# Sketched attention and a tanh-shrink FFN: weight loads cast by GpSimd's DMAs, fillers planned at the cold clock, more loads in flight

## The chip, the cores and the metric

The kernel runs on one core of a Trainium2 chip. The metric is device time in microseconds (us) of one execution, as the median of several. Shorter is better. The engines are TensorE (PE in the profile; PEld is its weight load), VectorE (DVE), ScalarE (ACT), GpSimd (POOL) and SyncE (SP). They run side by side, each through its own list of instructions in order, and wait for one another by semaphores. DMAs are issued by SP, ACT or POOL and carried out by 16 DMA engines that all of them share.

## The reference, cut to what matters

There are 4 batches of 4 heads, 1088 tokens each, 32 values per head. Queries and keys are sketched by two 8x32 matrices; the feature map is the outer product of the two sketches (64 features). Attention is linear: one 64x32 matrix per head is made from all keys and values, and each query is multiplied by it and divided by a denominator. The result, 4352 tokens x 128 values, goes through an FFN of width 2048.

```python
def phi(x):
    a = np.einsum('rd,bhsd->bhsr', S1, x)
    b = np.einsum('rd,bhsd->bhsr', S2, x)
    return np.einsum('bhsi,bhsj->bhsij', a, b).reshape(*x.shape[:-1], r * r)
q_p, k_p = (phi(q), phi(k))
kv = np.einsum('bhsf,bhsd->bhfd', k_p, v)
z = np.sum(k_p, axis=2)
num = np.einsum('bhsf,bhfd->bhsd', q_p, kv)
den = np.einsum('bhsf,bhf->bhs', q_p, z)[..., None] + 1e-06
x = (num / den) in token order, [4352, 128]
h = x @ w_in                    # 128 x 2048
out = (h - np.tanh(h)) @ w_out  # 2048 x 128
```

All inputs and the output are float32 in memory. The kernel uses bfloat16 for the FFN.

## The kernel before, in words

**A program that plans itself.** The kernel first collects operations with `P.add` (engine and estimated time, what is read and written, a priority `key`). `schedule` (line 103) then plays them through with these estimates: at each step it takes, over all engines, the operation that could start first, and among those of one engine that could start at nearly the same time the one with the lowest key. The order that results on each engine is what is emitted; on the chip each engine keeps to it and only waits where a semaphore makes it. So an estimate that is off does not change what is computed, but it can put an operation that must wait ahead of one that could run. A load's planned landing (lines 176 to 180) is the end of its transfer, at a given rate on one shared line, plus a constant.

**Loads.** `load` (line 409) issues one DMA; it also makes it wait until an older load has landed, so that with all the loads issued after that one no more than `IN_FLIGHT` bytes are on their way. There are three limits: for the first batch, for the weights, and for the other batches. The order is: S1 and S2, then k, q and v of batch 0 (`kL`, `qL`, `vL`; k in two halves, q in two pieces, v in four), then W_in and W_out in four DMAs each (256 KB, float32 into `wi_f`, `wo_f`), then k, v, q of batches 1 to 3. Nearly all of them are issued by SP; part of the first k by ACT.

**Weights** (`weights`, line 846). GpSimd copies the eight float32 quarters to bfloat16 (`wi`, `wo`). TensorE transposes W_in (L856), ScalarE copies that out of PSUM (`wiT`, L861), and 16 matmuls form W_in W_out (L868), which is kept as a bfloat16 head and rest (`wch`, `wcl`). With it h W_out is x (W_in W_out), so that only the tanh goes through the second FFN matmul.

**Attention of batch 0** (`attention_first`, line 815) is cut finely so that FFN columns come early. VectorE transposes k (L579), TensorE sketches it (`k_first`, L586), ScalarE copies the sketches (`abk`, L589). VectorE forms their outer products `w` (`k_outer`, L654); TensorE forms the Gram matrix of the sketches (L618), from which the denominator follows (L626), and the sum over tokens of `w` times v (`kv_mm`, L684 or L669), which is copied and transposed into `kvb` (L701). For q: transpose (L556), sketch (L601), divide (L743 to L751), outer product `qp` (L769), transpose `qpT` (L774), product with `kvb` (L785), and copies into `xT` in bfloat16 (L792, L795; they show as L324).

**Batches 1 to 3** do the same with other tilings: k transpose (L545), sketch (L570), transposes back into `abk` (L561), and q by L556, L723, L728, L731. `ORDER` sets how the k and q parts of the batches follow one another in priority.

**FFN** (`ffn`, line 877). The 4352 columns are ten groups: 256, 384, 448, six of 512, and 192. In a group, for each of 16 blocks of W_in: one matmul (L887) into one of four PSUM banks, one tanh on ScalarE (L890), and one matmul with W_out (L900) accumulated in one bank, with two matmuls by `wch` and `wcl` (L904) in between; then a transpose on VectorE (L909) and the output DMAs (L919). FFN work of finished columns fills TensorE between the attention steps.

**Fillers** (`fill`, line 200). Where the plan has TensorE free for over 0.35 us, and until the FFN's output bank is first used, matmuls of zeros (`zz`, L378) are put in, so that TensorE is not idle. They are planned at 216 ns each.

Of the kernel before, what the change touches and what calls it, by code (L numbers as in the profile page):

```python
# [6 lines left out]
DM = 128  # L7
DFF = 2048
# [51 lines left out]
class _Prog:  # L60
# [42 lines left out]
    def schedule(self, filler=None):  # L103
# [33 lines left out]
        while n < len(self.ops):  # L137
# [61 lines left out]

    def fill(self, filler, a, b):  # L200
        t = a
        while t + 450.0 < b:
            o = _Op()
            o.engs = {"tensor": (216.0, 215.0)}
            o.fn, o.key, o.dma, o.name, o.mode = filler[0], 0, 0, "fill", "128x128"
            o.deps, o.users, o.vals = {filler[1]: True}, [], []
            o.filler = True
            o.eng, o.t0, o.t1, o.lat = "tensor", t, t + 216.0, 215.0
# [86 lines left out]
def bass_polysketch_attn__then__act_tanh_shrink_kernel(  # L295
# [21 lines left out]
    def sbv(name, shape, dtype=FP32):  # L317
        return _Val(ap=sb(name, shape, dtype))
# [90 lines left out]
    def load(key, o_, i_, w, nbytes, eng="sync", rate=320.0):  # L409
        need, j = nbytes, len(flight)  # L410
        while j > 0 and need + flight[j - 1][1] <= limit[0]:
            j -= 1
            need += flight[j][1]
        o = P.add({eng: (450.0, 0.0)}, lambda e, n: e.dma_start(out=o_, in_=i_), w=w, key=key, dma=nbytes / rate,  # L414
                  after=[flight[j - 1][0]] if j > 0 else ())
        flight.append((o, nbytes))
        return o
# [28 lines left out]
    def load_v(key, b, eng="sync"):  # L446
        for g in range(4):
            w_ = (9 if g < 3 else 7) * 32
            vs = v[b].rearrange("h (t c) d -> t h (c d)", c=NC)[:, :, g * 288:g * 288 + w_]
            load(key + g, vL[b][g * 32:(g + 1) * 32, :, 0:w_], vs, [vvals[b][g]], 128 * w_ * 4, eng, rate=230.0)  # L450
# [6 lines left out]
    wif = [_Val(ap=wi_f[:, i * 512:(i + 1) * 512]) for i in range(4)]  # L457
    wof = [_Val(ap=wo_f[:, i * 4:(i + 1) * 4, :]) for i in range(4)]
    wos = moe_w_out.rearrange("(jb ji) c -> ji jb c", jb=NJB, ji=128)

    def load_wi(key, i):
        load(key, wif[i].ap, moe_w_in[:, i * 512:(i + 1) * 512], [wif[i]], 128 * 2048)

    def load_wo(key, i):
        load(key, wof[i].ap, wos[:, i * 4:(i + 1) * 4, :], [wof[i]], 128 * 2048)

    lk = iter(range(-90000, -80000, 10))
    load_k(next(lk), 0)
# [1 line left out]
    load_q(next(lk), 0, 1)  # L470
    load_v(next(lk), 0)
    limit[0] = IN_FLIGHT[1]
    for i in range(4):
        load_wi(next(lk), i)
    for i in range(4):
        load_wo(next(lk), i)
    limit[0] = IN_FLIGHT[2]
    for b in range(1, B):
        load_k(next(lk), b)
# [364 lines left out]
            q_piece(b, 0, *p, *st)  # L844

    def weights():
        for i in range(4):
            P.add(_g(512), lambda e, n, i=i: copy(e, n, wi[i].ap[:, :], wif[i].ap), r=[wif[i]], w=[wi[i]], key=-1000 + i, name=f"wi{i}")
        for i in range(4):
            last = P.add(_g(512), lambda e, n, i=i: copy(e, n, wo[i].ap[:, :, :], wof[i].ap), r=[wof[i]],  # L850
                         w=[wo[i]], key=T_FIRST + 100 + i, name=f"wo{i}")
        for i in range(2):
            tp = _Val(bank_h)
            for j in range(8):
                jb = i * 8 + j
                P.add(_pe(60), lambda e, n, tp=tp, j=j, jb=jb: e.transpose(  # L856
                    tp.ap.bitcast(BF16)[:, j * 128:(j + 1) * 128],
                    wi[jb // 4].ap[:, (jb % 4) * 128:(jb % 4 + 1) * 128], identb.ap[:, :]),
                    r=[wi[jb // 4], identb], w=[tp], key=T_FIRST + 1000 + 4000 * i, mode="128x128", name=f"wit{jb}")
            for z in range(2):  # L860
                P.add(_a(512), lambda e, n, tp=tp, i=i, z=z: e.copy(  # L861
                    wiT[i].ap.rearrange("p j c -> p (j c)")[:, z * 512:(z + 1) * 512],
                    tp.ap.bitcast(BF16)[:, z * 512:(z + 1) * 512]),
                    r=[tp], w=[wiT[i]], key=T_FIRST + 1000 + 4000 * i, name=f"wiT{i}")
        wc = _Val(bank_h)
        prev = None
        for jb in range(16):
            prev = P.add(_pe(60), lambda e, n, jb=jb: e.matmul(  # L868
                wc.ap[:, 0:128], wiT[jb // 8].ap[:, jb % 8, :], wo[jb // 4].ap[:, jb % 4, :],
                start=(jb == 0), stop=(jb == 15)), r=[wiT[jb // 8], wo[jb // 4]], w=[wc],  # L870
                key=T_FIRST + 6000, chain=prev, mode="128x128",
                after=[last], name=f"wc{jb}")
        P.add(_a(128), lambda e, n: e.copy(wch.ap[:, :], wc.ap[:, 0:128]), r=[wc], w=[wch], key=-60000.0, name="wch")
        P.add(_vp(128), lambda e, n: e.tensor_tensor(out=wcl.ap[:, :], in0=wc.ap[:, 0:128], in1=wch.ap[:, :],
                                                     op=ALU.subtract), r=[wc, wch], w=[wcl], key=-60000.0, name="wcl")

    def ffn(gi, c0, n_):
# [6 lines left out]
        for jb in range(NJB):  # L884
            hv, th = _Val(bank_h), _Val(th_p)
            ths.append(th)
            P.add(_pe(n_ / 2.4 + 2.6), lambda e, n, jb=jb, hv=hv: e.matmul(  # L887
                hv.ap[:, 0:n_], wi[jb // 4].ap[:, (jb % 4) * 128:(jb % 4 + 1) * 128], xt, start=True, stop=True),
                r=[wi[jb // 4]] + xs, w=[hv], key=t0 + jb * step, mode="128x128", name=f"h{gi}.{jb}")
            P.add(_a(n_), lambda e, n, hv=hv, th=th: e.activation(  # L890
                out=th.ap[:, 0:n_], in_=hv.ap[:, 0:n_], func=AF.Tanh, scale=-1.0),
                r=[hv], w=[th], key=t0 + jb * step, name=f"th{gi}.{jb}")
# [4 lines left out]
        for i, (kind, x) in enumerate(seq):  # L897
            st, sp_ = i == 0, i == len(seq) - 1
            if kind == "t":
                fn = lambda e, n, x=x, st=st, sp_=sp_: e.matmul(  # L900
                    ov.ap[:, 0:n_], wo[x // 4].ap[:, x % 4, :], ths[x].ap[:, 0:n_], start=st, stop=sp_)
                rd = [wo[x // 4], ths[x]]
# [104 lines left out]
```

## Time and profile before

| | |
|---|---|
| time, median of 3 runs | 115.92 us (115.78 to 116.11) |
| the profiled execution | 116.18 us, of which its span 114.1 us |
| TensorE busy | 104.7 us (92%) |
| ScalarE busy | 84.3 us (74%) |
| VectorE busy | 68.3 us (60%) |
| GpSimd busy | 8.3 us (7%) |
| read from HBM, written | 8.81 MB, 2.23 MB |
| mean granted TensorE clock | 0.985 |

The span runs from the first to the last instruction on the core. An L number is a line of the kernel. In a timeline row stand the start, the duration, the engine, line and operation, the tiles (out <- in), their form, how many were merged, and in brackets how long the engine was idle before and what released it. A "q" after an engine's name is its sequencer, where DMAs are issued. The granted clock is a share of TensorE's full clock; the record begins with the first change that was noted. A busy TensorE may be a slow one, or one working on zeros.

### The profile page before, as it was taken

The page shows a single profiled execution, that of the slowest core. Times are in us where ns is not written, and L with a number is a line of the kernel's source. Part 1 is how long each engine was busy: PE and PEld are TensorE (multiplying, and loading weights), DVE is VectorE, ACT ScalarE, POOL GpSimd, SP SyncE. Part 2 cuts the span into 40 slices and gives each one's busy share as a digit, 9 for nine tenths or more (in the row PEclk, how much of TensorE's full clock was granted, in tenths as well). Part 3 has the DMA queues.
Part 4 walks back from the last instruction along what each step waited for, and adds up shares of the span by engine and source line. Part 5 has one row for each costly group of instructions (what it writes and reads, how often), then busy time and mean ns, then how long its engine had stood idle before and what let it go on. Part 6 is the DMA issues. An engine that isn't in the chain of part 4 may idle for free.

```text
span 114.1 us, 3367 instructions
## 1 busy us (share of the span) xinstructions
PE 104.7 (92%) x1421; PEld 51.6 (45%) x1421; DVE 68.3 (60%) x111; ACT 84.3 (74%) x204; POOL 8.3 (7%) x28
## 2 busy tenths in 40 slices
PE   5999998894699999999999999999999999999990
PEld 2364883563554445543346343434423433434360
DVE  6639889944977999997999932999020020020200
ACT  3002259975149596987798968999799999999970
POOL 5300365300000000000000000000000000000000
PEclk9999999999859999999999999999999999999999
DMA  3797889738886966100220050014002305002352
GB/s 79 167 256 163 293 238 283 204 80 281 234 230 174 231 159 149 25 0 6 39 41 6 0 86 11 0 25 67 6 0 38 54 11 81 3 12 43 46 85 41
DMA packets 26575, 11.26 MB, mean 99 GB/s; under 512 B 19264, under 2 KB 24384, under 8 KB 26560
## 3 DMA queue, kind: packets, MB, share of 16 engines
q1 hardware_dynamic: 25600, 10.74, 40.5%
q10 hardware_dynamic: 960, 0.31, 1.2%
q8 instruction: 11, 0.18, 0.7%
q14 instruction: 4, 0.03, 0.1%
HBM read 8.81 MB, written 2.23 MB: 97 GB/s over the span
## 4 chain that ended last, share of the span: by engine, by line
PE 46%; DMA 20%; ACT 19%; DVE 8%; SPq 3%; issue 1%
ACT th L890 18%; PE pso L900 16%; PE psh L887 14%; DMA qL<-in_q_dram 8%; DMA kL<-in_k_dram 5%; PE psa L785 4%; DMA wi_f<-in_moe_w_in_dram 3%; DMA wo_f<-in_moe_w_out_dram 3%; SPq L414 3%; PE pso L904 3%; PE psa L684 2%; PE psa L669 2%; PE psa L723 2%; DVE w L654 2%; DVE ot L909 1%; DVE abk L561 1%
## 5 line engine op out<-in xcount | busy, mean ns | idle before, releaser
L890 ACT ACTIVATE th<-psh 128x512 bf16<-128x512 f32 (+4 forms) x160 | 71.3, 606 | 5.0 <-PE psh L887 4.5
L887 PE MATMUL psh<-xT,wi 128*128 128x512 bf16 (+4 forms) x160 | 52.9, 352 | 1.1 <-ACT th L890 0.3
L900 PE MATMUL pso<-th,wo 128*128 128x512 bf16 (+4 forms) x160 | 47.6, 348 | 0.4 <-DVE ot L909 0.4
L887 PEld LDWEIGHTS psh<-xT,wi 128*128 128x128 bf16 x160 | 15.4, 97 | 20.4 <-ACT th L890 9.1
L909 DVE STREAM_TRANSPOSE ot<-pso 128x512 f32<-128x512 f32 (+4 forms) x10 | 6.3, 630 | 28.9 <-PE pso L900 28.9
L900 PEld LDWEIGHTS pso<-th,wo 128*128 128x128 bf16 x160 | 14.8, 97 | 17.3 <-ACT th L890 4.3
L774 DVE STREAM_TRANSPOSE qpT<-qp 128x768 f32<-128x768 f32 (+1 forms) x14 | 12.0, 858 | 0.4
L769 DVE TENSOR_TENSOR qp<-ap,abc 128x768 f32<-128x768 f32 (+1 forms) x14 | 12.1, 867 | 0.1
L654 DVE TENSOR_TENSOR w<-abk 128x768 f32<-128x768 f32 (+2 forms) x12 | 10.9, 952 | 1.5 <-ACT abk L589 1.4
L785 PE MATMUL psa<-qpT,kvb 32*32 32x128 f32 (+4 forms) x336 | 8.3, 309 | 0.8 <-ACT th L890 0.3
L378 PE MATMUL pso<-zz 128*128 128x512 bf16 x21 | 7.8, 527 | 1.3 <-DVE zz L377 1.3
L785 PE MATMUL psh<-qpT,kvb 32*32 32x128 f32 (+4 forms) x112 | 8.3, 310 | 0.0
L556 DVE STREAM_TRANSPOSE qT<-qL 128x576 f32<-128x576 f32 (+3 forms) x8 | 5.6, 724 | 3.8 <-DMA qL<-in_q_dram 3.8
L785 PEld LDWEIGHTS psa<-qpT,kvb 32*32 32x32 f32 x336 | 5.2, 103 | 3.8 <-DVE qpT L774 2.1
L589 ACT COPY abk<-psa 128x256 f32<-128x256 f32 (+1 forms) x2 | 0.8, 400 | 6.0 <-PE psa L586 6.0
L324 ACT CAST xT<-psh 128x96 bf16<-128x96 f32 (+3 forms) x7 | 2.0, 290 | 4.0 <-PE psh L785 3.9
L378 PEld LDWEIGHTS pso<-zz 128*128 128x128 bf16 x21 | 2.6, 132 | 4.9 <-issue 3.3
L545 DVE STREAM_TRANSPOSE kT<-kL 128x576 f32<-128x576 f32 (+1 forms) x6 | 4.1, 715 | 0.6 <-DMA kL<-in_k_dram 0.6
L728 DVE STREAM_TRANSPOSE abc<-psh 128x288 f32<-128x288 f32 x3 | 1.4, 483 | 4.8 <-PE psh L723 4.7
L324 ACT CAST xT<-psa 128x64 bf16<-128x64 f32 (+4 forms) x11 | 4.2, 427 | 0.0
L785 PEld LDWEIGHTS psh<-qpT,kvb 32*32 32x32 f32 x112 | 3.9, 103 | 0.0
L618 PE MATMUL psa<-abk 128*32 128x32 f32 x72 | 1.5, 201 | 2.5 <-DVE abk L561 2.4
(72 smaller groups left out, 84.5 us busy)
## 6 DMA issues: line engine op xcount, KB each, us to landing
vL<-in_v_dram SPq DMA_DIRECT2D x12, 144.0 KB, 4.5
wi_f<-in_moe_w_in_dram SPq DMA_DIRECT2D x4, 256.0 KB, 3.7
wo_f<-in_moe_w_out_dram SPq DMA_DIRECT2D x4, 256.0 KB, 4.1
out_dram<-ot SPq DMA_DIRECT2D x16, 64.0 KB, 2.0
kL<-in_k_dram SPq DMA_DIRECT2D x3, 288.0 KB, 3.7
qL<-in_q_dram SPq DMA_DIRECT2D x3, 288.0 KB, 3.9
kL<-in_k_dram SPq DMA_DIRECT2D x3, 256.0 KB, 4.2
qL<-in_q_dram SPq DMA_DIRECT2D x3, 256.0 KB, 4.2
```

What stands on the lines that cost most here:

```text
L324: return e.copy(o, i) if name == "scalar" else e.tensor_copy(o, i)
L378: filler = (lambda e, n: e.matmul(bank_o.slots[0][0][:, 0:512], zz.ap[:, 0:128], zz.ap[:, 128:640], start=True, stop=True), zop, bank_o)
L545: P.add(_v(hi - lo), lambda e, n, lo=lo, hi=hi: e.transpose(kT[b].ap[:, lo:hi], kL[b][:, lo:hi]), r=[kvals[b][i]], w=[kT[b]], key=nk(), na ...
L556: P.add(_v((z - a) * 32), lambda e, n: e.transpose(qTs[b][:, a * 32:z * 32], val.ap), r=[val], w=tvs, key=nk(), name=f"qT{b}.{i}")
L654: P.add(_v(nx * 64), lambda e, n: e.tensor_tensor(out=wv.ap[:, 0:nx * 64].rearrange("p (x i j) -> p x i j", i=8, j=8), in0=abh(0)[:, :, :, ...
L769: P.add(_v(cn * 256), lambda e, n, qp=qp, c0=c0, cn=cn: e.tensor_tensor(out=qp.ap[:, 0:cn * 256].rearrange("p (x i j) -> p x i j", i=8, j= ...
L774: P.add(_v(cn * 256), lambda e, n, qp=qp, o0=o0, cn=cn: e.transpose(qt.ap[:, o0 * 256:(o0 + cn) * 256], qp.ap[:, 0:cn * 256]), r=[qp], w=[ ...
L785: i = e.matmul(banks[g].ap[h * 32:(h + 1) * 32, 0:nb * 32], kvb.ap[g * 32:(g + 1) * 32, x, h * 32:(h + 1) * 32], qq[g * 32:(g + 1) * 32, 0 ...
L887: P.add(_pe(n_ / 2.4 + 2.6), lambda e, n, jb=jb, hv=hv: e.matmul(hv.ap[:, 0:n_], wi[jb // 4].ap[:, (jb % 4) * 128:(jb % 4 + 1) * 128], xt, ...
L890: P.add(_a(n_), lambda e, n, hv=hv, th=th: e.activation(out=th.ap[:, 0:n_], in_=hv.ap[:, 0:n_], func=AF.Tanh, scale=-1.0), r=[hv], w=[th], ...
L900: fn = lambda e, n, x=x, st=st, sp_=sp_: e.matmul(ov.ap[:, 0:n_], wo[x // 4].ap[:, x % 4, :], ths[x].ap[:, 0:n_], start=st, stop=sp_)
L909: P.add(_vp(n_), lambda e, n: e.transpose(ot.ap[:, 0:n_], ov.ap[:, 0:n_]), r=[ov], w=[ot], key=-60000, name=f"ot{gi}")
```

## The change

Three things are edited, with the estimates that go with them.

- The limits of bytes in flight for the weights and for batches 1 to 3 go from 1.1 to 1.6 million.
- W_in and W_out are loaded by four DMAs of 512 KB of float32, issued by GpSimd, that write bfloat16 straight into `wib` and `wob`. Their readers wait for halves (`wih`, `woh`) instead of quarters. The eight GpSimd copies are gone, and so is the extra wait of the W_in W_out matmuls for the last of them.
- A filler that is planned to start before 6.3 us is planned at 427 ns.
- The plan's estimates change: a DMA issued by GpSimd takes 1.1 us of its queue; v is planned at 205 bytes/ns (230 before), W_out at 260 (320 before); the constant after a transfer is 1.2 us for S1 and S2, 0.7 for the first batch and the first half of W_in, and 1.5 for all others (before: 0.6 for all up to batch 2's loads).

Since the plan's estimates change, the order on every engine can change too.

```diff
-IN_FLIGHT = [4000000, 1100000, 1100000]
+IN_FLIGHT = [4000000, 1600000, 1600000]
...
-                o.t1 = dma_free + (600.0 if o.key < -89800 else 1500.0)
+                o.t1 = dma_free + (1200.0 if o.key < -95000 else 700.0 if o.key < -89950 else 1500.0)
...
     def fill(self, filler, a, b):
         t = a
-        while t + 450.0 < b:
+        while True:
+            occ = 427.0 if t < 6300.0 else 216.0
+            if t + occ + 230.0 > b:
+                break
             o = _Op()
-            o.engs = {"tensor": (216.0, 215.0)}
+            o.engs = {"tensor": (occ, 215.0)}
...
-    wi_f = sb("wi_f", [128, DFF])
-    wo_f = sb("wo_f", [128, NJB, DM])
-    wi = [sbv("wi", [128, 512], BF16) for _ in range(4)]
-    wo = [sbv("wo", [128, 4, DM], BF16) for _ in range(4)]
+    wib = sb("wi", [128, DFF], BF16)
+    wob = sb("wo", [128, NJB, DM], BF16)
+    wih = [_Val(ap=wib[:, i * 1024:(i + 1) * 1024]) for i in range(2)]
+    woh = [_Val(ap=wob[:, i * 8:(i + 1) * 8, :]) for i in range(2)]
...
-        o = P.add({eng: (450.0, 0.0)}, lambda e, n: e.dma_start(out=o_, in_=i_), w=w, key=key, dma=nbytes / rate,
+        o = P.add({eng: (1100.0 if eng == "gpsimd" else 450.0, 0.0)}, lambda e, n: e.dma_start(out=o_, in_=i_), w=w, key=key, dma=nbytes / rate,
...
-            load(key + g, ..., eng, rate=230.0)
+            load(key + g, ..., eng, rate=205.0)
...
-    for i in range(4):
-        load_wi(next(lk), i)
-    for i in range(4):
-        load_wo(next(lk), i)
+    for i in range(2):
+        load(next(lk), wih[i].ap, moe_w_in[:, i * 1024:(i + 1) * 1024], [wih[i]], 128 * 4096, "gpsimd")
+    for i in range(2):
+        load(next(lk), woh[i].ap, wos[:, i * 8:(i + 1) * 8, :], [woh[i]], 128 * 4096, "gpsimd", rate=260.0)
...
-        for i in range(4):
-            P.add(_g(512), lambda e, n, i=i: copy(e, n, wi[i].ap[:, :], wif[i].ap), r=[wif[i]], w=[wi[i]], key=-1000 + i, name=f"wi{i}")
-        for i in range(4):
-            last = P.add(_g(512), lambda e, n, i=i: copy(e, n, wo[i].ap[:, :, :], wof[i].ap), r=[wof[i]],
-                         w=[wo[i]], key=T_FIRST + 100 + i, name=f"wo{i}")
...
-                after=[last], name=f"wc{jb}")
+                name=f"wc{jb}")
```

In the matmuls that read weights only the names of the buffers change.

More of the change, by code (lines that the diff above doesn't have):

```diff
@@ L449, in load_v @@
             vs = v[b].rearrange("h (t c) d -> t h (c d)", c=NC)[:, :, g * 288:g * 288 + w_]
-            load(key + g, vL[b][g * 32:(g + 1) * 32, :, 0:w_], vs, [vvals[b][g]], 128 * w_ * 4, eng, rate=230.0)
+            load(key + g, vL[b][g * 32:(g + 1) * 32, :, 0:w_], vs, [vvals[b][g]], 128 * w_ * 4, eng, rate=205.0)
     def load_q(key, b, i):
@@ L868, in weights @@
             prev = P.add(_pe(60), lambda e, n, jb=jb: e.matmul(
-                wc.ap[:, 0:128], wiT[jb // 8].ap[:, jb % 8, :], wo[jb // 4].ap[:, jb % 4, :],
-                start=(jb == 0), stop=(jb == 15)), r=[wiT[jb // 8], wo[jb // 4]], w=[wc],
+                wc.ap[:, 0:128], wiT[jb // 8].ap[:, jb % 8, :], wob[:, jb, :],
+                start=(jb == 0), stop=(jb == 15)), r=[wiT[jb // 8], woh[jb // 8]], w=[wc],
                 key=T_FIRST + 6000, chain=prev, mode="128x128",
-                after=[last], name=f"wc{jb}")
+                name=f"wc{jb}")
         P.add(_a(128), lambda e, n: e.copy(wch.ap[:, :], wc.ap[:, 0:128]), r=[wc], w=[wch], key=-60000.0, name="wch")
@@ L900, in ffn @@
                 fn = lambda e, n, x=x, st=st, sp_=sp_: e.matmul(
-                    ov.ap[:, 0:n_], wo[x // 4].ap[:, x % 4, :], ths[x].ap[:, 0:n_], start=st, stop=sp_)
-                rd = [wo[x // 4], ths[x]]
+                    ov.ap[:, 0:n_], wob[:, x, :], ths[x].ap[:, 0:n_], start=st, stop=sp_)
+                rd = [woh[x // 8], ths[x]]
             else:
```

16 lines of the change are left out of this document (5 added, 11 removed).

## The prediction

> **What bounds the kernel now.** First the windows view, cut where the limit changes (columns: stretch, length, busy time and count by engine, granted TensorE clock, DMA share, GB/s).
>
> ```profile
> span 114.1 us, 3367 instructions
> 17.00:30.00 13.00, 9.48 (x220) 5.82 (x217) 9.62 (x15) 9.69 (x32) 2.81 (x4) 1.00 0.76 216
> 30.00:34.00 4.00, 4.00 (x90) 2.45 (x88) 3.59 (x6) 1.41 (x4) 0.00 (x0) 0.57 0.85 222
> 50.00:82.00 32.00, 31.64 (x476) 13.57 (x474) 24.95 (x37) 27.44 (x61) 0.00 (x0) 1.00 0.17 26
> 82.00:101.00 19.00, 18.65 (x81) 7.13 (x80) 2.15 (x3) 19.00 (x41) 0.00 (x0) 1.00 0.19 28
> ```
>
> From 50 to 82 us TensorE is never free (31.64 of 32), from 82 to 101 ScalarE is not (19.00 of 19): a fixed amount of work is fed through, and it ends earlier by as much as it starts earlier or loses less on the way. The losses are early: 3.5 us of TensorE idle between 17 and 30, and four microseconds at 0.57 of the clock just after. So I looked at the order of events around 27 us, in the chain of waits, the timeline and TensorE's waits.
>
> ```profile
> 23.86 3.35 DMA qL<-in_q_dram
> 23.26 1.37 DVE L545 STREAM_TRANSPOSE kT<-kL 128x576 f32<-128x576 f32 x2 [0.57 <-DMA kL<-in_k_dram]
> 26.41 0.55 PE L868 MATMUL psh<-wo,wiT 128*128 128x128 bf16 x7
> 27.23 1.37 DVE L556 STREAM_TRANSPOSE qT<-qL 128x576 f32<-128x576 f32 x2 [2.60 <-DMA qL<-in_q_dram]
> 29.39 0.38 PE L618 MATMUL psa<-abk 128*32 128x32 f32 x18 [2.42 <-DVE abk L561]
> ```
>
> VectorE has an order written ahead. In it the transpose of batch 1's q stands before the `abk` transposes of batch 1's k, so VectorE waits 2.60 us for q, and the Gram matmuls behind `abk` wait 2.42 us. The q load was issued only at 23.86, when an older load had landed. The idle TensorE is then clocked down: in 30 to 34 the loss is 4 x (1 - 0.57) = 1.72 us. Together the late load costs 4.14 us.
>
> The other end is the first FFN matmul, and what precedes it.
>
> ```profile
> 4.71 1.50 DVE L579 STREAM_TRANSPOSE kT<-kL 128x512 f32<-128x512 f32 x2
> 1.25 6.17 PE L378 MATMUL pso<-zz 128*128 128x512 bf16 x16 [1.25 <-DVE zz L377]
> 7.26 2.12 PE L586 MATMUL psa<-wk,kT 128*128 128x64 f32 x18
> 8.71 2.73 DVE L654 TENSOR_TENSOR w<-abk 128x1024 f32<-128x1024 f32 x3 [1.39 <-ACT abk L589]
> 17.30 0.39 PE L887 MATMUL psh<-xT,wi 128*128 128x256 bf16 x2
> ```
>
> The first half of k is transposed by about 5.45 (4.71 plus half of 1.50), but its sketch starts at 7.26, because 16 fillers, planned at 0.216 us each, take 6.17 us. VectorE then waits 1.39 us at L654.
>
> **Part 1, fillers.** They are now planned at 0.427 us before 6.3 us. From the old matmul at 1.25, nine of them end near 5.1, so the sketch can start at 5.45. The old trace shows when the array gets fast: fillers follow one another every 0.43 us until
>
> ```profile
> 5.92 0.15 PEld L378 LDWEIGHTS pso<-zz 128*128 128x128 bf16 x1 [0.28 <-issue]
> 6.35 0.58 PEld L378 LDWEIGHTS pso<-zz 128*128 128x128 bf16 x3 [0.28 <-issue]
> 6.87 0.45 DVE L556 STREAM_TRANSPOSE qT<-qL 128x256 f32<-128x256 f32 x1 [0.66 <-DMA qL<-in_q_dram]
> ```
>
> and 0.19 apart from 6.35. With the same moment, the 18 sketch matmuls (0.118 each, 2.12 / 18) run four or so at double length until 6.35 and the other 14 in 1.65, ending near 8.0 instead of 9.38. The first ScalarE copy comes out as much earlier, and L654 starts when VectorE has finished the q transpose at 7.32: at 7.35 instead of 8.71, **-1.36 us** for the VectorE chain. Bounds: 0 (the clock stays low, a rival below) and -1.8 (7.26 - 5.45).
>
> **Part 2, no GpSimd copies.** Eight casts leave GpSimd; it has nothing else to do then, so their own time is worth nothing. But VectorE gains:
>
> ```profile
> 13.13 2.81 POOL L324 CAST wi<-wi_f 128x512 bf16<-128x512 f32 x4 [8.01 <-DMA wi_f<-in_moe_w_in_dram]
> 13.85 1.05 DVE L769 TENSOR_TENSOR qp<-ap,abc 128x512 f32<-128x512 f32 x1
> 19.97 0.65 DVE L769 TENSOR_TENSOR qp<-ap,abc 128x512 f32<-128x512 f32 x1
> 13.43 0.39 DVE L751 TENSOR_TENSOR ap<-abc,rd 128x64 f32<-128x64 f32 x1
> 12.67 0.23 DVE L743 TENSOR_TENSOR m<-abc 128x64 f32<-128x64 f32 x1 [0.18 <-ACT abc L606]
> ```
>
> The same product takes 1.05 beside a cast and 0.65 later, and the small one 0.39 against 0.23 for one of its size before the casts: 0.40 + 0.16 = **-0.56** ahead of 17.30. Bounds 0 and -0.56.
>
> **Part 3, loads.** The weights are four DMAs of 512 KB on GpSimd's queue. By the limit of 1.6 MB the first waits for the first piece of q (landed by 6.87, row above), the second for the first piece of v, the third for the last piece of v, the fourth for the first weights. Behind them GpSimd has only its final waits. On SP the loads of batch 1 now wait: k for the second half of W_in and the first of W_out, q for the second half of W_out and for k. Before, q (288 KB) + v (544) + half of k (256) = 1088 KB was already over 1.1 MB, hence the wait until 23.86. The sizes, and what the queue has to give:
>
> ```profile
> vL<-in_v_dram SPq DMA_DIRECT2D x12, 144.0 KB, 4.5
> qL<-in_q_dram SPq DMA_DIRECT2D x3, 288.0 KB, 3.9
> kL<-in_k_dram SPq DMA_DIRECT2D x3, 256.0 KB, 4.2
> vL<-in_v_dram SPq DMA_DIRECT2D x4, 112.0 KB, 4.7
> ...
> 9.44 2.62 SPq L414 DMA_DIRECT2D wi_f<-in_moe_w_in_dram  x4
> 9.00:11.00 2.00, 1.92 (x35) 0.94 (x34) 2.00 (x3) 0.61 (x2) 0.00 (x0) 1.00 0.56 141
> 11.00:19.00 8.00, 7.16 (x182) 5.64 (x180) 7.35 (x14) 3.94 (x13) 4.01 (x6) 1.00 0.94 267
> 19.00:26.00 7.00, 6.26 (x171) 3.72 (x170) 4.96 (x8) 6.16 (x22) 1.76 (x2) 1.00 0.60 170
> 12.21 1.05 PEld L684 LDWEIGHTS psa<-w,vL 128*32 128x32 f32 x72
> 14.89 0.38 ACT L324 COPY kvb<-psa 128x256 f32<-128x256 f32 x1
> 14.94 0.71 DVE L774 STREAM_TRANSPOSE qpT<-qp 128x512 f32<-128x512 f32 x1
> ```
>
> Idle DMA time: 2 x 0.44 + 8 x 0.06 + 7 x 0.40 = 4.2 us, of which 2.8 lie where the limit held q back. If all is used, q lands at 27.23 - 4.2 = 23.0; if none, at 27.23. I take 2.9 of it, near the row 19 to 26, so 24.3: the issues still wait for landings. No row shows a casting DMA, nor one issued by GpSimd. Half the bytes are written, so it could be twice as fast; then q is no longer late, VectorE's transposes up to 24.63 (23.26 + 1.37) are, and the stall is gone, no more. It could be half as fast: the slower rival. I take the rate of now, since as many bytes are read.
>
> The price: W_in starts at about 8 instead of after 9.44, beside v of batch 0. Two queues that share 2.2 us of transfer put v back by 0 to 1.1. Its matmuls (12.21) would like to start 1.9 earlier; what follows them, `kvb`, is done 0.4 before the `qpT` that is needed with it (15.27 against 15.65). So of 1.1 I charge **+0.7**. The first FFN matmul then comes 1.36 + 0.56 - 0.7 = **1.2 us earlier**, near 16.1.
>
> What is left of the stall: in the old order, q landing to Gram matmul is 29.39 - 27.23 = 2.16, so 24.3 + 2.16 = 26.46, against a TensorE that gets there at 26.96 - 1.2 = 25.76. The wait is 0.7 instead of 2.42: **-1.72**, with ends 0 and -2.42. The planner's landing times also become later and so nearer the trace, and may put `abk` first; I do not count it, for a new order brings waits of its own. Waits of this size do not clock the array down between 17 and 30:
>
> ```profile
> PEld psh L887 <- ACT th L890: 9.1, 28, 0.5
> ```
>
> (28 waits, the longest 0.5; clock 1.00 in the row of 17 to 30). So the slow stretch goes too: **-1.72**, ends 0 and -1.72.
>
> **Sum.** The profiled execution took 116.18 us: the span of 114.1 and 2.1 around it. 116.18 - 1.2 - 1.72 - 1.72 = 111.5. It is 0.26 over the median of 115.92, so for the median **111.3 us**.
>
> **The rivals.**
>
> *The loads come no earlier, or the wait only moves.* For it: from 11 to 19 the queue is already 0.94 busy, and a reordered program can wait elsewhere, say for a half of W_in where a quarter sufficed. Against it: 0.60 from 19 to 26. The stall and the slow clock stay, the early start is kept: 115.92 - 1.2 = 114.7.
>
> *The clock stays low after the start.* Fewer fillers and a gap before the sketch could leave the array slow for another stretch as long as that of 30 to 34. The sketch then takes 4.24 from 5.45 and ends at 9.7, 0.3 after the old one: 1.36 + 0.3 are lost, 113.0. For it: matmuls after a pause ran slow at 30. Against it: the gap is at most 0.4 us. The Trainium skill ("TensorE: Matmul & The Clock Gate", "What's actually happening") says the array speeds up after one busy window of about 3.4 us that runs freely; the 1.25 to 6.35 us of the fillers agrees, and by that rule this rival hangs on where the window falls.
>
> *Slower: the casting DMAs are slow.* One mechanism: the cast halves the rate of the four weight DMAs. Now 2.1 MB move at about 267 GB/s (row 11 to 19), 7.9 us; at half they take 15.7. That is 7.8 us more, less the 2.9 recovered: q lands 4.9 after 27.23. At worst the end moves as far, 120.8; at best, if the order has FFN work to put there, by nothing; the middle is 118.4. It decides as soon as the four DMAs need over 11 us (7.9 + 2.9). Against it: nothing in the trace; for it: no row shows a cast. The Trainium skill ("DMA: Bandwidth & Descriptors", "Specifications") has transfers below 512 B as read-modify-write; W_out's rows of 128 values are written as 256 B. By this rule half of that slowdown would come; no run here shows it.
>
> **How the numbers follow.** Forecast 0.58; loads no earlier 0.15; low clock 0.13; slow casts 0.14. The forecast's own range goes from 109.5 (no stall at all, no price for v: 111.3 - 0.7 - 0.7, rounded down) to 113. For 8 in 10 I take 109.5 to 115.0, which holds the two middle cases and leaves out the slow one and a little on either side. This kernel's runs differ by 0.3%, so that is the limit of "same": faster 0.82 (forecast, low clock, nearly all of the first rival), same 0.04, slower 0.14.
>
> **What would show it.** Nine or ten fillers ending near 5.1, and the sketch at 5.5 with the granted fast clock from about 6.4; `qp` at 0.65 on its first use; first FFN matmul near 16; batch 1's q transposed near 24 to 25, the wait at L618 under 1 us, and clock 1.00 from 17 on. Wrong would be: a TensorE idle time of 2 us or more anywhere before 40, weights landing after 18 us, or an unchanged end in spite of a start gained, which would mean that ScalarE or VectorE sets the middle.

## The result, and the profile after

| | before | after |
|---|---|---|
| median of four runs, us | 115.91 (115.78 to 116.11) | 112.05 (111.4 to 112.53) |
| profiled execution, us | 116.18 | 112.28 |
| its span, us | 114.1 | 110.1 |

The changed kernel takes 0.966 of the time (95% interval 0.961 to 0.972): 3.9 us less. Runs of one kernel differ by several us here, in part because the granted clock falls for a stretch in some and not in others, so the ratios below use only the runs within 1.5% of the fastest of their kernel (of the kernel before, 2 of 11, 14 of 23 and 4 of 11 in the three series), and the medians use all. Line numbers shift in the changed kernel: the Gram matmuls are L613 (L618 before), the first FFN matmul L877 (L887), k's transposes back into `abk` L556 (L561), q's transpose L551 (L556).

First the windows view of the changed kernel, in the columns of the prediction (stretch, length, busy time and count of PE, PEld, DVE, ACT, POOL, granted clock, DMA share, GB/s).

```profile
11.00:19.00 8.00, 6.79 (x171) 6.11 (x170) 4.65 (x12) 3.03 (x10) 2.00 (x3) 0.79 1.07 146
17.00:30.00 13.00, 12.23 (x346) 7.87 (x346) 10.89 (x18) 10.18 (x34) 0.00 (x0) 1.00 0.97 243
30.00:34.00 4.00, 4.00 (x75) 2.12 (x75) 3.91 (x8) 3.03 (x8) 0.00 (x0) 1.00 0.99 285
```

From 17 to 30 TensorE is busy for 12.23 of 13 us instead of 9.48, and the stretch from 30 to 34 has the full clock instead of 0.57. But a slow stretch has appeared where there was none: 0.79 from 11 to 19. The timeline of TensorE shows how it comes about.

```profile
1.26 3.60 PE L381 MATMUL pso<-zz 128*128 128x512 bf16 x8 [1.26 <-DVE zz L380]
5.08 2.48 PE L581 MATMUL psa<-wk,kT 128*128 128x64 f32 x18 [0.23 <-DVE wk L496]
10.35 0.69 PE L596 MATMUL psa<-wq,qT 128*128 128x96 f32 x4 [1.36 <-DVE wq L634]
12.05 2.15 PE L679 MATMUL psa<-w,vL 128*32 128x64 f32 x72 [1.01 <-DMA vL<-in_v_dram]
18.30 0.39 PE L877 MATMUL psh<-xT,wi 128*128 128x256 bf16 x2
27.32 0.38 PE L613 MATMUL psa<-abk 128*32 128x32 f32 x18
```

The sketch starts at 5.08 instead of 7.26. Then TensorE waits 1.36 us for `wq` and 1.01 us for v, the clock halves, and the 72 matmuls with v take 2.15 us (1.21 in an execution without the fall, shown below). The first FFN matmul comes at 18.30, **1.0 us later** than before. The Gram matmuls of batch 1 start at 27.32 instead of 29.39, with no wait. VectorE's timeline shows why.

```profile
12.75 0.69 DVE L764 TENSOR_TENSOR qp<-ap,abc 128x512 f32<-128x512 f32 x1
26.36 0.85 DVE L556 STREAM_TRANSPOSE abk<-psa 128x288 f32<-128x288 f32 x2 [1.61 <-PE psa L565]
27.25 2.70 DVE L649 TENSOR_TENSOR w<-abk 128x768 f32<-128x768 f32 x3
29.86 0.77 DVE L551 STREAM_TRANSPOSE qT<-qL 128x576 f32<-128x576 f32 x1
```

`abk` and `w` now stand **ahead** of q's transpose. VectorE no longer waits for q here; it waits 1.61 us for TensorE's sketch, while TensorE has FFN work. The new estimates have changed the order, which the prediction declined to count. Whether this swap is what brings the gain is a question for the experiments.

The ten transposes of the FFN's output, one per group, mark how far the work has come (the view of one tile: duration least/median/most, first and last start). Before, then after:

```profile
L909 DVE STREAM_TRANSPOSE ot<-pso x10: 383/706/717, 34.4 to 111.0; 128x512 f32<-128x512 f32 x6, 128x256 f32<-128x256 f32 x1, 128x384 f32<-128x384 f32 x1, 128x448 f32<-128x448 f32 x1
```

```profile
L899 DVE STREAM_TRANSPOSE ot<-pso x10: 383/716/719, 31.3 to 106.7; 128x512 f32<-128x512 f32 x6, 128x256 f32<-128x256 f32 x1, 128x384 f32<-128x384 f32 x1, 128x448 f32<-128x448 f32 x1
```

So the account of the two profiled executions is: +1.0 at the first FFN matmul, -4.1 from there to the first group's end (34.4 - 17.30 = 17.1 against 31.3 - 18.30 = 13.0), and -1.2 from there to the last group's end (76.6 against 75.4). Together -4.3; the span, which ends with the output's DMAs, is 4.0 shorter.

The loads, on the page of before and of after (queue: packets, MB, share of the 16 engines; issues: KB each, us to landing) and in the timeline of after:

```profile
q1 hardware_dynamic: 25600, 10.74, 40.5%
```

```profile
span 110.1 us, 3329 instructions
...
q1 hardware_dynamic: 22912, 8.64, 35.3%
q0 software_dynamic: 2368, 1.05, 8.1%
...
wi<-in_moe_w_in_dram POOLq DMA_DIRECT2D x2, 256.0 KB, 4.6
wo<-in_moe_w_out_dram POOLq DMA_DIRECT2D x2, 256.0 KB, 6.2
```

```profile
8.06 0.74 POOL L417 DMA_DIRECT2D wi<-in_moe_w_in_dram  x1 [2.58 <-DMA qL<-in_q_dram]
10.69 0.55 POOL L417 DMA_DIRECT2D wi<-in_moe_w_in_dram  x1 [1.89 <-DMA vL<-in_v_dram]
12.29 1.77 POOL L417 DMA_DIRECT2D wo<-in_moe_w_out_dram  x2 [1.06 <-DMA vL<-in_v_dram]
...
21.46 0.91 SPq L417 DMA_DIRECT2D qL<-in_q_dram  x2
```

The weights' casting DMAs took 0.081 x 110.1 = 8.9 us of all 16 engines. Taking the weights out of the old queue saved 0.405 x 114.1 - 0.353 x 110.1 = 7.3 us. So the cast costs 1.6 us of DMA time. The trace's packets show where (medians): 2048 bytes of W_in took 84 ns in float32, and 173 ns where 4096 were read and 2048 written, which is the same per byte read; 512 bytes of W_out took 27 ns, and 41 ns where 256 were written, which is 1.5 times. The last weight landed at 19.71 (19.90 before). q of batch 1 was issued at 21.46 instead of 23.86, and its two pieces landed at 25.97 and 26.63 (27.21 and 27.87).

### The profile page after: what moved, and what is told of

It is laid out like the page before. It is cut to its first block, busy times and chain, and to the rows that moved or that the text cites. A ratio compares the mean times of both kernels' runs of the same rounds, so it can differ in the third digit from the quotient of the medians.

```text
span 110.1 us, 3329 instructions
## 1 busy us (share of the span) xinstructions
PE 100.4 (91%) x1403; PEld 51.3 (47%) x1412; DVE 67.0 (61%) x111; ACT 83.7 (76%) x204; POOL 5.5 (5%) x24
## 3 DMA queue, kind: packets, MB, share of 16 engines
q0 software_dynamic: 2368, 1.05, 8.1%
## 4 chain that ended last, share of the span: by engine, by line
PE 59%; ACT 26%; DMA 6%; SPq 4%; issue 1%; DVE 0%
ACT th L880 22%; PE pso L890 18%; PE psh L877 18%; DMA vL<-in_v_dram 6%; PE psa L780 6%; SPq L417 4%; PE psa L679 3%; ACT xT L327 3%; PE pso L894 2%; PE psh L596 2%; PE psa L664 2%; PE psa L565 2%; ACT wiT L851 2%; PE psa L718 1%; PE psh L858 1%
## 5 line engine op out<-in xcount | busy, mean ns | idle before, releaser
L877 PE MATMUL psh<-xT,wi 128*128 128x512 bf16 (+4 forms) x155 | 50.8, 348 | 1.3 <-ACT th L880 0.6
L890 PE MATMUL pso<-th,wo 128*128 128x512 bf16 (+4 forms) x157 | 46.8, 348 | 0.8 <-issue 0.6
L877 PEld LDWEIGHTS psh<-xT,wi 128*128 128x128 bf16 x160 | 15.3, 97 | 20.5 <-ACT th L880 8.4
L764 DVE TENSOR_TENSOR qp<-ap,abc 128x768 f32<-128x768 f32 (+1 forms) x14 | 11.4, 813 | 0.1
L551 DVE STREAM_TRANSPOSE qT<-qL 128x576 f32<-128x576 f32 (+3 forms) x8 | 5.7, 721 | 1.6 <-DMA qL<-in_q_dram 1.6
L381 PE MATMUL pso<-zz 128*128 128x512 bf16 x11 | 4.6, 563 | 1.3 <-DVE zz L380 1.3
L679 PE MATMUL psa<-w,vL 128*32 128x64 f32 x144 | 3.8, 269 | 1.0 <-DMA vL<-in_v_dram 1.0
L738 DVE TENSOR_TENSOR m<-abc 128x288 f32<-128x288 f32 (+2 forms) x5 | 1.9, 382 | 3.1 <-ACT abc L601 3.0
L679 PEld LDWEIGHTS psa<-w,vL 128*32 128x32 f32 x144 | 3.1, 141 | 1.5 <-DMA vL<-in_v_dram 1.2
```

The lines of the kernel that those rows point to most:

```text
L381: filler = (lambda e, n: e.matmul(bank_o.slots[0][0][:, 0:512], zz.ap[:, 0:128], zz.ap[:, 128:640], start=True, stop=True), zop, bank_o)
L551: P.add(_v((z - a) * 32), lambda e, n: e.transpose(qTs[b][:, a * 32:z * 32], val.ap), r=[val], w=tvs, key=nk(), name=f"qT{b}.{i}")
L679: i = e.matmul(bk[2].ap[h * 32:(h + 1) * 32, 0:64], vL[b][:, h, blk * 32:(blk + 1) * 32], wvs[b, p].ap[:, (bi * 4 + h) * 64:(bi * 4 + h + ...
L764: P.add(_v(cn * 256), lambda e, n, qp=qp, c0=c0, cn=cn: e.tensor_tensor(out=qp.ap[:, 0:cn * 256].rearrange("p (x i j) -> p x i j", i=8, j= ...
L890: fn = lambda e, n, x=x, st=st, sp_=sp_: e.matmul(ov.ap[:, 0:n_], wob[:, x, :], ths[x].ap[:, 0:n_], start=st, stop=sp_)
```

## The experiments

All twelve runs stand in one table first (us; e1 and h1 are the same kernel, and a1 and h2 are the changed one; "clock" is the number of runs whose mean granted clock was 0.99 or more).

| run | what it is | median (range) | clock | ratio to before, 95% |
|---|---|---|---|---|
| e1, h1 | before + new load estimates only | 111.17 and 111.49 (110.62 to 112.25) | 10 of 12 | 0.977 (0.961 to 0.993), 0.978 (0.971 to 0.985) |
| a1, h2 | the changed kernel again | 113.03 and 112.23 (110.33 to 113.93) | 6 of 12 | 0.959 (0.953 to 0.964), 0.977 (0.964 to 0.989) |
| o1 | after, old load estimates | 114.66 (112.83 to 117.78) | 5 of 6 | 0.985 (0.979 to 0.992) |
| s1 | before, one swap on VectorE | 115.09 (113.29 to 116.96) | 6 of 12 | 0.989 (0.985 to 0.994) |
| f1 | before + new filler rule | 115.33 (114.14 to 116.9) | 5 of 12 | 0.996 (0.992 to 1.001) |
| e2 | after, old filler rule | 111.72 (110.99 to 117.77) | 5 of 6 | 0.979 (0.967 to 0.992) |
| e3 | after + fillers in two gaps | 114.37 (110.97 to 117.37) | 2 of 6 | 0.976 (0.943 to 1.009) |
| e4 | after, 1.1 MB for batches 1 to 3 | 111.93 (110.69 to 112.58) | 2 of 6 | 0.979 (0.962 to 0.995) |
| b1 | e1 + 1.6 MB in flight | 111.81 (111.33 to 112.08) | 5 of 6 | 0.980 (0.974 to 0.986) |
| b2 | e1 + twelve first fillers, not 17 | 111.4 (111.28 to 112.46) | 5 of 6 | 0.980 (0.972 to 0.987) |

The kernel before ran beside them at medians of 115.35 (e1 to e4), 115.69 (s1, o1, f1, a1) and 115.98 us (h1, h2, b1, b2). Its 45 runs lie between 113.18 and 117.55, a far wider spread than the 0.3% that the prediction took from the first chip. They kept the clock at 0.99 or more in 11 of 45, with a median of 114.64 in these 11; the ten such runs of e1 and h1 have 111.35. So some 3.3 us of the gain are there where both kept the clock.

**The new estimates alone (e1).** The theory was that the new order, and not the three parts, removes the stall. The edit to before is three lines of estimates that only the planner uses; 1.1 MB in flight, float32 loads, GpSimd copies and the old filler rule stay.

```diff
-                o.t1 = dma_free + (600.0 if o.key < -89800 else 1500.0)
+                o.t1 = dma_free + (1200.0 if o.key < -95000 else 700.0 if o.key < -89950 else 1500.0)
-            load(key + g, ..., eng, rate=230.0)
+            load(key + g, ..., eng, rate=205.0)
-        load(key, wof[i].ap, ..., [wof[i]], 128 * 2048)
+        load(key, wof[i].ap, ..., [wof[i]], 128 * 2048, rate=260.0)
```

> The kernel before with the plan's new estimates alone (landing constants, rates of v and W_out): fillers, float32 weight loads by SP, GpSimd copies and 1.1 MB in flight stay. VectorE's order becomes that of the changed kernel (abk and w of batch 1 ahead of its q transposes). Theory ORDER (the gain came from that order, not from earlier loads): the 2.4 us wait of TensorE at the Gram matmuls and the slow clock after it are gone, first FFN matmul still near 17.3 us: about 111.8 us. Theory LOADS (q and k of batch 1 had to come earlier): 115 us or more. It also tells what the other parts are worth together: if it is at or under 112.0, nothing.

It took 111.17 us, as little as the changed kernel (h1, beside it in one series: 111.49 against 112.23). VectorE's and ScalarE's orders came out the same as the changed kernel's. The planner now has q's first piece landing at 23.6 us instead of 20.7, and so starts `w` first, at 22.7. VectorE's timeline around 27 us, the first FFN matmul and the ends of the groups:

```profile
25.83 0.85 DVE L561 STREAM_TRANSPOSE abk<-psa 128x288 f32<-128x288 f32 x2 [1.15 <-PE psa L570]
29.33 0.77 DVE L556 STREAM_TRANSPOSE qT<-qL 128x576 f32<-128x576 f32 x1
```

```profile
17.74 0.39 PE L887 MATMUL psh<-xT,wi 128*128 128x256 bf16 x2
L909 DVE STREAM_TRANSPOSE ot<-pso x10: 383/716/718, 30.8 to 106.1; 128x512 f32<-128x512 f32 x6, 128x256 f32<-128x256 f32 x1, 128x384 f32<-128x384 f32 x1, 128x448 f32<-128x448 f32 x1
```

q landed at 27.29, no earlier than before, and nobody waited for it. From the first FFN matmul (17.74) to the first group's end (30.81) it is 13.1 us, as after; in h1 it is 13.0. The whole -4.1 is there without any of the three parts.

**The three parts with the old estimates (o1).** The reverse: after, with the old constants and rates, so that VectorE keeps q ahead of `abk`, as the prediction assumed.

```diff
-                o.t1 = dma_free + (1200.0 if o.key < -95000 else 700.0 if o.key < -89950 else 1500.0)
+                o.t1 = dma_free + (600.0 if o.key < -89800 else 1500.0)
-        o = P.add({eng: (1100.0 if eng == "gpsimd" else 450.0, 0.0)}, ...
+        o = P.add({eng: (450.0, 0.0)}, ...
-            load(key + g, ..., eng, rate=205.0)
+            load(key + g, ..., eng, rate=230.0)
-        load(next(lk), woh[i].ap, ..., "gpsimd", rate=260.0)
+        load(next(lk), woh[i].ap, ..., "gpsimd")
```

> The changed kernel (fillers, casting DMAs, 1.6 MB in flight) with the old estimates: VectorE's order has batch 1's q transposes first again. Theory ORDER: TensorE waits for abk until 1.2 us after q's landing, which was 26.6, so 28.5 to 29, and the clock falls: 114.5 to 116. Theory LOADS: the three parts bring the gain by themselves, 112.

In its profiled execution the predicted mechanism runs nearly to the number. VectorE's timeline, then TensorE's:

```profile
24.43 1.37 DVE L551 STREAM_TRANSPOSE qT<-qL 128x576 f32<-128x576 f32 x2 [1.90 <-DMA qL<-in_q_dram]
```

```profile
16.63 0.38 PE L877 MATMUL psh<-xT,wi 128*128 128x256 bf16 x2
26.58 0.38 PE L613 MATMUL psa<-abk 128*32 128x32 f32 x18 [0.63 <-DVE abk L556]
```

q is there at 24.4 (forecast 24.3), the Gram matmuls start at 26.58 (26.46) after a wait of 0.63 (0.7), and no slow stretch follows. This was the fastest execution of six, 112.83 us, 3.35 less than the profiled one of before, and its q is the earliest of all profiles, so that it fits the forecast this closely is partly luck. The median is only 1.0 below before's in the same series: the other five lie between 113.49 and 117.78, four of them with the clock at 0.997 or above, and where they lost time no profile shows. Where the clock stayed at 0.99 or more, the median is 114.31 (five runs) against 114.64 of before (three in the series).

**One swap on VectorE (s1).** Is it enough to move batch 1's q behind `w`, with everything else in the order of before?

```diff
     P.schedule(filler)
+    ve = P.order["vector"]
+    late_q = [o for o in ve if o.name in ("qT1.0", "qT1.1")]
+    ve = [o for o in ve if o not in late_q]
+    at = 1 + [o.name for o in ve].index("w1.2")
+    ve[at:at] = late_q
...
```

> The kernel before with one edit of its finished order: on VectorE the two q transposes of batch 1 stand behind the abk transposes and the products w instead of ahead of them. No other instruction, load, filler or engine changes. Theory ORDER: Gram matmuls near 26.9 instead of 29.4, no slow clock after them, 3.5 to 4 us faster than before, about 112. Theory LOADS: q is still late, the wait goes to its sketch, at most 1 us is gained: 115.

It took 115.09 us, 0.6 under before; the 112 of theory ORDER did not come. The stall is gone as intended, but the timeline and the waits of TensorE show two new ones behind it:

```profile
26.59 0.38 PE L618 MATMUL psa<-abk 128*32 128x32 f32 x18
30.38 0.28 PE L904 MATMUL pso<-xT,wcl 128*128 128x256 bf16 x1 [0.51 <-DVE wcl L874]
```

```profile
PE psa L570 <- DVE abc L731: 1.2, 1, 1.2
```

```profile
33.47 1.37 DVE L556 STREAM_TRANSPOSE qT<-qL 128x576 f32<-128x576 f32 x2 [1.54 <-DMA qL<-in_q_dram]
```

```profile
L909 DVE STREAM_TRANSPOSE ot<-pso x10: 383/706/717, 31.5 to 109.0; 128x512 f32<-128x512 f32 x6, 128x256 f32<-128x256 f32 x1, 128x384 f32<-128x384 f32 x1, 128x448 f32<-128x448 f32 x1
```

The first group ends 2.9 earlier than before, the last only 2.0. The row of VectorE shows where the longer wait comes from: `abc` stands behind the q transposes of the next batch, and these wait 1.54 us for their load. It is the same kind of stall as before, one batch later. The full order of e1 also moves the later steps, and keeps the gain (30.8 to 106.1); which of its other moves counts for how much was not tested.

**The filler rule alone (f1).** Before, with the new `fill`, shown in the change.

> The kernel before with the new planning of fillers alone; every other instruction in the old order. My prediction's part 1: 1.2 us faster than before. Theory now: the sketch starts at 5.1 instead of 7.3, but v of batch 0 lands at 11.7 as before and the k-v matmuls cannot start much sooner; with longer idle times the clock may fall between 9 and 16: no gain, 0.5 us faster to 1 us slower.

115.33 us: no difference from before that can be told. TensorE's timeline:

```profile
1.25 3.59 PE L381 MATMUL pso<-zz 128*128 128x512 bf16 x8 [1.25 <-DVE zz L380]
5.34 4.10 PE L589 MATMUL psa<-wk,kT 128*128 128x64 f32 x18 [0.50 <-DVE kT L582]
13.04 1.21 PE L687 MATMUL psa<-w,vL 128*32 128x64 f32 x72
```

The sketch starts at 5.34, 1.9 earlier than before, and takes 4.10 us instead of 2.12: the array stayed slow, until 12.78 by the trace, and the matmuls with v came 0.8 later than before. The short run of fillers had not made it fast in this execution.

**The old filler rule in the changed kernel (e2).** The rest of the order is the same.

```diff
-        while True:
-            occ = 427.0 if t < 6300.0 else 216.0
-            if t + occ + 230.0 > b:
-                break
+        while t + 450.0 < b:
+            occ = 216.0
```

> The changed kernel with fillers planned at 216 ns throughout, as before; every other instruction in the same order. My prediction's part 1 (shorter filler run brings the start forward): 1.2 us slower than the changed kernel, 113.2. Theory CLOCK (the shorter run leaves TensorE idle at 9 to 10.4 and 11 to 12, and the clock low from 12.1 to 15.5, while v of batch 0 lands near 12 in any case): the clock stays at 1.00 or falls elsewhere, first FFN matmul near 17.3 instead of 18.3: 111.0.

111.72 us, with the full clock in five of six runs. In its profile the sketch comes at 6.32 and the first FFN matmul at 17.47, 0.8 before that in the changed kernel's first profile. No gain of the new rule shows here either, though the changed kernel did not run in this series. A wait shows that no semaphore explains:

```profile
16.64 0.24 PE L778 MATMUL psa<-qpT,kvb 32*32 32x64 f32 x1 [1.01 <-issue]
```

**Fillers in the two gaps (e3).** Five fillers ahead of the first q sketch and four ahead of the matmuls with v, to keep the clock up.

```diff
+                more = {"qsk0.0": 5, "kvmm0.0": 4}.get(o.name, 0)
+                if more:
+                    self.fill(filler, 7000.0, 7000.0 + 216.0 * more + 231.0)
```

> The changed kernel with nine more fillers, five ahead of the first q sketch and four ahead of the first k-v matmuls of batch 0, where TensorE waited 1.4 and 1.0 us; the order is otherwise the same. Theory CLOCK: granted clock 1.00 from 12 to 16, the 72 k-v matmuls in 1.2 us instead of 2.15, first FFN matmul near 16.8, 110.5 us. Rival (the landing of v and then of the weights sets the start): clock up, but first FFN matmul no earlier than 18.0, 111.9.

114.37 us with a spread of 6.4: it settles nothing for the median. In the profile the clock fell twice. The windows view, with the two stretches ahead of a fall in the first and second row, and the timeline at the second:

```profile
4.22:7.63 3.41, 2.71 (x21) 2.19 (x20) 2.41 (x7) 0.37 (x1) 1.31 (x5) 1.00 0.90 233
...
28.00:31.50 3.50, 1.91 (x68) 1.46 (x66) 2.85 (x4) 0.70 (x4) 0.00 (x0) 1.00 1.05 270
31.50:35.00 3.50, 3.50 (x51) 2.28 (x40) 1.54 (x4) 1.82 (x5) 0.00 (x0) 0.51 0.47 148
```

```profile
30.77 0.44 PE L861 MATMUL psh<-wo,wiT 128*128 128x128 bf16 x5 [1.59 <-issue]
```

The first fall, at 7.63, was ahead of the added fillers. The second followed 1.59 us of waiting for nothing that the profile shows.

**1.1 MB in flight, in the new order (e4) and 1.6 MB in the order of e1 (b1).** In both the order is planned as it was and only the loads' waits are exchanged afterwards: e4 holds batches 1 to 3 of the changed kernel to 1.1 MB, b1 gives e1 the 1.6 MB. The core of both, where `alt` holds the load that the planner's limit waits for and the one that the new limit waits for:

```diff
+REAL = [4000000, 1600000, 1100000]
...
     P.schedule(filler)
+    for o in P.ops:
+        if o.alt is not None:
+            if o.alt[0] is not None:
+                o.deps.pop(o.alt[0])
+            if o.alt[1] is not None:
+                o.deps.setdefault(o.alt[1], False)
```

(In b1 the last limit is 1600000.)

> The changed kernel, its order of instructions kept exactly, with the loads of batches 1 to 3 held to 1.1 MB in flight again (the weights keep 1.6). Theory ORDER: q of batch 1 lands some 2 us later, near 28 to 29, but is only wanted at 29.9: 112.0, at most 0.5 more. Theory LOADS: the later q and v cost what the limit had brought, 113.5 or more.

> The estimates alone, with 1.6 MB in flight for the weights and for batches 1 to 3, the weights in float32 by SP and copied by GpSimd as before; the order of instructions is that of the estimates alone exactly. Theory PLAN: q of batch 1 lands 1 to 3 us earlier but is not waited for: 111.2, no change. Rival: the earlier v and q bring up to 1 us: 110.2. v of batch 0 may land up to 1 us later, beside the weights.

111.93 and 111.81 us (112.05 and 111.49 without the edit, e4 in another series): no worth of the limit shows in either direction. In b1 q landed at 25.74, 1.6 earlier than in e1, and the last group ended at 106.1, as in e1. In e4 it landed at 25.22, not near 28 as expected but earlier than in the changed kernel's first profile, so e4 does not show what a late q would do; e1, with 27.29 in the same order of VectorE, does.

**Fewer fillers in the order of e1 (b2).** At most twelve in the first run, five fewer than the 17 of e1.

```diff
-        while t + 450.0 < b:
+        n = 0
+        while t + 450.0 < b and (n < 12 or a > 2000.0):
+            n += 1
```

> The estimates alone, with 12 fillers instead of 17 ahead of the first k sketch; everything else in the same order. Twelve end near 6.3 us. If the start sets the end as my prediction had it and the clock still rises in time: sketch at 6.4 instead of 7.5, 110.2. If v's landing sets the k-v matmuls: 111.0. If the clock rises a window later: 112.

111.4 us, beside 111.49 for e1's order run again in the same series. The sketch starts at 6.15 instead of 7.48, and the matmuls with v wait for v:

```profile
6.15 2.12 PE L588 MATMUL psa<-wk,kT 128*128 128x64 f32 x18
11.92 1.21 PE L686 MATMUL psa<-w,vL 128*32 128x64 f32 x72 [1.23 <-DMA vL<-in_v_dram]
```

That is 11.92 against 11.95 in e1: the earlier sketch is given back to v at once. The first FFN matmul still came at 16.97, 0.8 before e1's, but the last group ended at 106.3, 0.2 after e1's.

**The changed kernel and the estimates again (a1, h2, h1).** These repeat the changed kernel twice and e1 once.

> The changed kernel itself, for comparison with the others on this chip: 112.0. The moment at which the granted clock falls and rises should differ from one profile to the next.

> The kernel with the new estimates alone, once more, beside the changed kernel on one chip. Theory PLAN (the new estimates' order on all engines makes the gain; fillers, casts and bytes in flight add nothing that can be measured): 111.2, within 0.6 of the changed kernel or faster than it. Rival PARTS (the three parts are worth 1 us or more on top): over 1 us slower than the changed kernel.

> The changed kernel, for the comparison: 112.0 by both theories. By theory PLAN its runs spread more than those with the estimates alone, since its short filler run leaves it to chance when the clock rises and falls: 110.4 to 114 against 110.6 to 112.3.

a1's profiled execution, 110.58 us, had no fall of the clock. TensorE's timeline:

```profile
9.48 0.69 PE L596 MATMUL psa<-wq,qT 128*128 128x96 f32 x4 [0.50 <-DVE wq L634]
11.00 1.21 PE L679 MATMUL psa<-w,vL 128*32 128x64 f32 x72 [0.83 <-DMA vL<-in_v_dram]
15.88 0.38 PE L877 MATMUL psh<-xT,wi 128*128 128x256 bf16 x2
```

```profile
L899 DVE STREAM_TRANSPOSE ot<-pso x10: 383/716/718, 29.6 to 105.0; 128x512 f32<-128x512 f32 x6, 128x256 f32<-128x256 f32 x1, 128x384 f32<-128x384 f32 x1, 128x448 f32<-128x448 f32 x1
```

The first FFN matmul is at 15.88 (forecast 16.1), 2.4 before that of the first profile, and both group ends come 1.7 before. Not all of this is the clock: v landed at 10.95 instead of 12.01, so 1.05 of the 2.4 us are there when the 72 matmuls start. The other 1.4 are left for the fall. h2's profiled execution is like the first: the clock fell at 11.41, the FFN began at 17.92.

In the same series e1's order took 111.49 and the changed kernel 112.23 us. Their intervals overlap, so no version is shown to beat the changed kernel. But the estimates alone are not shown to be slower either, and they spread less (1.6 us over both series against 3.6).

## Why the prediction came out

**The sum** was 111.3 us against 112.05 measured, within the range of 109.5 to 115.0. It was right for reasons that are only partly the predicted ones: an early term of the forecast failed, and an effect that was set aside made up for it. That the two came to nearly the same sum is luck.

**Part 1, fillers (-1.36, bounds 0 and -1.8).** Eight fillers (nine were forecast) end at 4.86 and the sketch starts at 5.08 (5.45). In a1 the step then ran as worked out: `w` started on VectorE at 7.27, for 7.35 forecast. What failed is the step behind it, that TensorE stays busy enough for the clock; this rival was given only 0.13. It happened, in another place than described: not between fillers and sketch but in the two waits that the earlier start opened, for `wq` and for v. It cost 1.4 us up to the first FFN matmul, against 1.36 + 0.3 priced. Of 16 runs of the changed kernel 7 kept the clock at 0.99 or more. In the new order the old rule kept it in 20 of 24 runs (e1, h1, b1, e2), the new rule in 9 of 22 (the changed kernel and e4). That points to the fillers, but o1, with the new rule in the old order, kept it in 5 of 6 too, so the fillers alone do not decide it. What f1 shows is the worth of the new rule by itself: nothing that can be told from none. In the first profile q's first piece, moreover, landed at 7.75 instead of 6.85, which the weights cannot have caused, since the first of them was issued behind it at 8.06.

**Part 2, VectorE beside the casts (-0.56).** The product took 0.69 instead of 1.05 on its first use, the small one 0.22 instead of 0.39: -0.53. The size was right, but VectorE no longer set the start. The chain of waits of the changed kernel comes from v:

```profile
5.63 6.38 DMA vL<-in_v_dram
12.05 2.15 PE psa L679 x72
```

**Part 3, the price of v (+0.7, from 0 to 1.1).** v landed at 12.01 in the first profile and 10.95 in a1, against 11.72 before: +0.3 and -0.8. The term was too high, but what is behind it counted more than foreseen: v's landing, and no longer VectorE's chain, sets the matmuls with v in the changed kernel, and it eats an earlier sketch (b2 shows it alone).

**The stall (-1.72 of 2.42) and the slow clock behind it (-1.72).** Measured from the first FFN matmul to the first group's end: -4.1 for -3.44 forecast. The step that failed is the assumption that VectorE keeps its old order. "I do not count it, for a new order brings waits of its own" set aside the very thing that did the work: e1 has all of the 4.1 us with q as late as ever. The mechanism that was predicted is real; o1 shows it at 24.4, 26.58 and 0.63 us. But by the medians the three parts together, with the start, are worth 1.0 us and not 4.6. The warning in that sentence holds for s1, where 2.9 us at the first group are 2.0 at the last and 0.6 in the median, not for the planner's full order. So what is shown is that the new order as a whole removes the stall; that the place of batch 1's q alone does it is not, for s1 speaks against it.

**What was not foreseen at all** is the -1.2 between the first and the last group's end. The ten transposes of the trace put it in two places: 0.7 between the first and the second, 0.6 between the third and the fourth. From the first to the last it is 75.3 to 75.7 us in nine of the ten profiles in the new order (e1: 75.3; b2 has 76.3), and 76.5 to 77.5 in the four in the old one (o1, before, s1, f1). So it comes with the new order as a whole.

**The other rivals.** *Loads no earlier*: half right. q came 1.2 earlier, not 2.9, and the weights only 0.2, past the 18 us that was named as a sign of error. One profile says little here: q's first piece landed between 25.17 and 27.29 in the six profiles with the old loads and limits, and between 24.41 and 25.97 in the six with the new ones, 1.4 earlier on average. The late q of before was in part a matter of chance, as s1 has the same loads and the 25.17. That the loads gained so little cost next to nothing, because q was no longer in front of anything; a1 alone shows a wait for `wo`, 0.8 us. *Slow casts*: the rate was not halved. W_in's packets kept their rate, W_out's took 1.5 times; 1.6 us of DMA time for the 7.8 of the rival. The Trainium skill ("DMA: Bandwidth & Descriptors", "Specifications") on transfers below 512 B agrees in direction with W_out's 256-byte writes; whether the read-modify-write is the reason no run here tells apart.

## What to carry to other kernels

Where a planner writes the order of the engines, compare its landing times with the trace before touching the loads: three lines of estimates gave here what the whole change gave. They did not have to be right for it: the planner's landing of q moved from 20.7 to 23.6 us, with 27.3 in the trace. To tell a mechanism from the order that comes with it, run the mechanism in the old order and the order without the mechanism. And do not shorten a warm-up to the length that one trace shows: an earlier start that opens gaps can cost as much in clock as it gains.

## What the runs showed of the hardware

**The clock falls without a long gap.** Each of the six slow stretches amid the work of the profiles lasts 3.41 us, at other moments in each execution (30.34 to 33.75 in before, 12.09 to 15.50 in the first one after). In three profiles of the same kernel (first, h2, a1) the step after the sketch had TensorE busy for this long (windows view of each; the first two fell at its end, the third did not):

```profile
8.68:12.09 3.41, 1.03 (x17) 0.81 (x19) 3.38 (x7) 0.33 (x2) 0.66 (x2) 1.00 0.85 141
```

```profile
7.99:11.41 3.42, 1.59 (x31) 1.13 (x32) 3.38 (x7) 0.50 (x2) 0.61 (x2) 1.00 0.99 172
```

```profile
9.30:12.71 3.41, 2.40 (x81) 2.15 (x82) 3.24 (x10) 0.69 (x2) 2.02 (x3) 1.00 0.91 124
```

With 1.03 and 1.59 us busy of 3.41 the clock fell, with 2.40 it did not; the longest single wait in the first was 1.36 us, in the second 1.65. The step ahead of the fall in the kernel before, which holds the stall, fits in:

```profile
26.92:30.34 3.42, 1.00 (x33) 0.76 (x32) 3.08 (x6) 0.70 (x3) 0.00 (x0) 1.00 0.81 225
```

So do e4 (1.59, then a fall), b2 (2.09) and b1 (2.13, no fall in either). The Trainium skill ("TensorE: Matmul & The Clock Gate", "Why this matters for your kernels") asks only for no idle gap above about 3 us. By that rule no fall would have come here; the measurement decides. Busy time alone does not settle it either: in e3 the clock fell after a step with 2.71 us busy, much of it the small float32 sketch. What exactly is counted stays open.

**TensorE waits that no semaphore explains.** e2 and e3 show 1.01 and 1.59 us put down to "issue", at places that shift when a few fillers are added or taken away. The packets of the traces hold a pattern: from 12 us on there are twelve such waits of 0.34 us or more, in nine of the profiles, and each is over 1.25 to 1.63 us after a 16 KB transfer of instructions on queue 8 ended (in e2 15.35 and 16.64, in e3 29.28 and 30.77). That suggests that the next instructions came late; no run tested it.
